# Nine of the third token block's twelve gated units computed from split operands, with the weight splits and the attention steps moved to fit

## The chip, the cores and the metric

The kernel runs on one core of a Trainium2 chip. The metric is device time in microseconds (us); lower is better. The core has a matrix engine (TensorE, PE in the profile; PEld is its weight load), a vector engine (VectorE, DVE), an activation engine (ScalarE, ACT), a general engine (GpSimd, POOL) and a queue that issues DMA transfers (SyncE, SP). Each takes its instructions in the order in which the program wrote them, and they wait for each other by semaphores.

## What is computed

The reference is an attention block with polynomial features, followed by a gated feed-forward block. The inputs are float64 in memory and arrive as pairs of 32-bit words.

```python
# attention: q, k, v are (4, 4, 1088, 32); S1, S2 are (8, 32)
phi(x) = outer(S1 @ x, S2 @ x)                 # 64 features of each token
kv = sum_s phi(k)_s v_s ;  z = sum_s phi(k)_s
attn = (phi(q) @ kv) / (phi(q) . z + 1e-6)
x = attn as (4352, 128)                        # heads side by side
# feed-forward: w_gate, w_val are (128, 1536); w_out is (1536, 128)
g = x @ w_gate
out = (g * sigmoid(g) * (x @ w_val)) @ w_out
```

## The kernel before

The 4352 tokens are cut into blocks: the first 1088 (batch 0) into three blocks, 0, 1 and 2, of 384, 320 and 384 tokens, the rest into blocks of up to 480. The 1536 hidden columns are twelve chunks of 128, so a block is twelve units (i, j): block i, chunk j. A unit multiplies the block's tokens with the gate and the value weights of its chunk, and joins the two results to a hidden tile. A down product (`down`, its matmul is L1077) multiplies a hidden tile with the chunk of `wo` and adds it to the block's sum in PSUM.

There are two forms of a unit:

- A plain unit (`unit`, L1025) is two float32 matmuls, then a Silu on ACT (L1029) and a product on DVE (L1040).
- A unit of parts (`start_unit` and `finish_unit`) splits tokens and weights into a high part, a scaled low part and their difference, and does six matmuls in the type fp32r: two of the differences (L989), a scaling of the PSUM pair on ACT (L992), four more on top (L1001, L1002), Silu (L1004) and product (L1009). The two sums of one unit lie in a pair of PSUM banks. There are three such pairs; `pair` takes the one that is longest unused and not held. A started unit holds its pair until its product.

For the second form the weights must have been split. The weights are cut for this into four groups of three chunks, called chunk 0 to 3 in the change: `cut_weights` makes g0 to g3 (gate) and v0 to v3 (value). Each is a generator of four steps: the high part on ACT (L843), the low part on DVE or POOL (L846), its scaling on ACT (L848), the difference on DVE (L851) or POOL (L855). `cut_tokens` splits the tokens of a block (ACT L865, DVE L873, DVE or POOL L868). `at` runs the next step of the ones named, and the tables `steps_at` say behind which unit or down product.

The weights themselves come as 64-bit words by DMA and are turned into float32 by `narrow` (DVE L263, L264, ACT, DVE L271, L277, POOL or DVE L286). The dictionary `parts` says behind which unit each such step is written.

The attention of batches 1 to 3 is one generator, `attentions`, and `parts_of(n)` advances it by n steps. For batch 1 the steps are: transposes of keys and queries (L327, L578, with the next batch's loads on SP), key products (L354), features on DVE (L377), their sums `zs` on POOL (L547), and in one step the key-value products (L388), the key products of batch 2 (L354), the products with `zs` (L713), a fold on DVE (L601 to L608) and the rotated copies `spread` by DMA (L729, L730). Then come the query sketches (L342), the query features and their transposes (DVE L377, L758), and last `numerators` (L776), which uses two PSUM pairs and writes the tokens of batch 1 (copies L793), the first that block 3 (`HEAD`) needs.

The order of the work around the change is written by hand, in one stream for each engine:

1. The loop over `seq` writes the plain units, index z. From z = 17 each is followed by a down product and one attention step. `lates` are hidden tiles whose product was put off; `catch_up` does it later.
2. The loop over n writes `ND` down products with attention steps, weight splits and the split of block 2's tokens ("x") between them.
3. The loop over j writes block 2's units of parts, each with a down product: start of unit j + 1, finish of unit j, down product.
4. The `while` loop writes the down products left. In it stand the numerators, the split of block 3's tokens and, with two down products left, the start of block 3's first unit.
5. Blocks 3 and on run in the loop over y, all in units of parts.

Of the kernel before, what the change touches and what calls it, by code (L numbers as in the profile page):

```python
# [19 lines left out]
def kernel(  # L20
# [28 lines left out]
    nc = tc.nc  # L49
    P = nc.NUM_PARTITIONS  # L50
# [8 lines left out]
    NCH = Dff // P  # L59
# [73 lines left out]
    def let_go(keep):  # L133
        i = kept.pop(keep)
        held.discard(i)
        touch(i, i + 1)
# [13 lines left out]
    wg = const.tile([P, NCH, P], FP32, name="wg")  # L150
    wv = const.tile([P, NCH, P], FP32, name="wv")
# [162 lines left out]
    slots = [(hbuf[:, k, :] if k < NH - NL else late[:, k - NH + NL, :]) for k in range(NH)]  # L314
# [482 lines left out]
    HEAD = len(steps)  # L797
    hidden = {}
    acc = {}
    todo = []  # L800
# [16 lines left out]
    def whole(ap):  # L817
        return ap.bitcast(FP32)
# [10 lines left out]
    def home(w, c):  # L829


        if w is wg:
            return [big("phq", k) if k < 4 else big("raw", k - 4) for k in range(3 * c, 3 * c + 3)]
        return [
            stage.tile([P, 3, P], F32R, tag=tag, name=name, bufs=6)[:]
            for tag, name in (("exp", "w1"), ("man", "wb"), (("exp", "man")[c % 2], "wd"))
        ]

    def cut_weights(w, c, low, engine):

        w1, wb, wd = w_parts[id(w), c] = home(w, c)
        src = w[:, 3 * c : 3 * c + 3, :]
        nc.scalar.activation(out=w1, in_=src, func=AF.Copy, scale=CUT)  # L843
        yield
        low = low[0]
        engine.tensor_tensor(out=low, in0=src, in1=whole(w1), op=ALU.subtract)  # L846
        yield
        nc.scalar.activation(out=wb, in_=low, func=AF.Copy, scale=BETA)  # L848
        yield
        if engine is nc.vector:  # L850
            nc.vector.scalar_tensor_tensor(  # L851
                out=wd, in0=low, scalar=-BETA, in1=whole(w1), op0=ALU.mult, op1=ALU.add
            )
        else:
            engine.tensor_tensor(out=wd, in0=whole(w1), in1=whole(wb), op=ALU.subtract)  # L855

    def cut_tokens(i, engine=nc.gpsimd, soon=False):

        t0, n = blocks[i]
        x = xT[:, t0 : t0 + n]  # L860
        x1, x0, xd = x_parts[i] = [
            apool.tile([P, WB], F32R, tag=tag, name=name, bufs=2)
            for tag, name in (("qb", "x1"), ("dT", "x0"), ("rd", "xd"))
        ]
        nc.scalar.activation(x1[:, 0:n], x, AF.Copy, scale=CUT)  # L865
# [33 lines left out]
    def now(where, y):  # L899
        for f in where.pop(y, ()):  # L900
            f()
# [81 lines left out]
    def start_unit(i, j):  # L983

        n = blocks[i][1]
        xd = x_parts[i][2][:, 0:n]
        ps = sums_of[i, j] = pair((i, j))[:, :, 0:n]
        for k, w in enumerate((wg, wv)):
            nc.tensor.matmul(  # L989
                ps[:, k], w_parts[id(w), j // 3][2][:, j % 3, :], xd, start=True, stop=True  # L990
            )
        nc.scalar.activation(ps, ps, AF.Copy, scale=-1.0 / WHOLE)  # L992

    def finish_unit(i, j, y=None):
        n = blocks[i][1]
        x1, x0, _ = (x[:, 0:n] for x in x_parts[i])
        ps = sums_of.pop((i, j))
        now(before, y)
        for k, w in enumerate((wg, wv)):
            w1, wb = (w_parts[id(w), j // 3][t][:, j % 3, :] for t in range(2))  # L1000
            nc.tensor.matmul(ps[:, k], w1, x1, start=False, stop=False, skip_group_check=True)  # L1001
            nc.tensor.matmul(ps[:, k], wb, x0, start=False, stop=True, skip_group_check=True)  # L1002
        sg = fpool.tile([P, WB], FP32, tag="sg", name="sg", bufs=5)[:, 0:n]
        nc.scalar.activation(sg, ps[:, 0], AF.Silu, scale=WHOLE)  # L1004
        slot_of[i, j] = slots.pop(0)
        hj = slot_of[i, j]
        hidden[i, j] = hj
        todo.append((i, j))
        nc.vector.scalar_tensor_tensor(  # L1009
            out=hj[:, 0:n], in0=ps[:, 1], scalar=WHOLE, in1=sg, op0=ALU.mult, op1=ALU.mult  # L1010
        )
        let_go((i, j))
        now(behind, y)
        if (i, j) in DOWN:
            cut_hidden(y, i, j)
# [135 lines left out]
    def part(name, i):  # L1151

        next(fills[name, i], None)
# [38 lines left out]
    order = [c for p in (c0, aside, c1) for c in range(*p)]  # L1192
# [8 lines left out]
    n = steps[0][1]  # L1201
# [92 lines left out]
    def free(c):  # L1294
        return [room[:, c, :].rearrange("p (c f) -> p c f", f=P)]

    w = ("wg", "wv")
    parts = {}
    for z, p in enumerate(both(3, *w) + both(4, *w) + [("wo", i) for i in range(4)]):
        z += z // 2 * 4  # L1300
        for t in (z, z + 1, z + 2 + z % 6):
            parts.setdefault(t, []).append(p)
    seq = [(0, 3), (0, 4), (0, 5), (2, 0), (2, 1), (2, 2)]
    seq += [(i, j) for i in (1, 2) for j in range(3, 6)]
    seq += [(i, j) for j0 in (6, 9) for i in (0, 1) for j in range(j0, j0 + 3)]
    order = [(0, j) for j in range(NCH)] + [(1, j) for j in range(3, NCH)] + [(1, j) for j in range(3)]

    lows = {}  # L1310
    cuts = {"x": cut_tokens(2, nc.vector, soon=True)}
    for c in (2, 3, 0, 1):
        cuts["g%d" % c] = cut_weights(wg, c, free(8 + c % 2), nc.vector if c else nc.gpsimd)
        lows["v%d" % c] = free(6 + c % 2)
        cuts["v%d" % c] = cut_weights(wv, c, lows["v%d" % c], nc.vector if c == 1 else nc.gpsimd)

    def at(*names):
        for name in names:
            next(cuts[name], None)
# [4 lines left out]
            todo.insert(0, order.pop(0))  # L1324
        down()

    steps_at = {20: ("v2",), 21: ("v3", "v2", "v3"), 22: ("g2",), 23: ("g3",)}
    for z, (i, j) in enumerate(seq):
        if z == 17:
            free_banks.pop()  # L1330
            turn[0] %= 4
        unit(i, j)
        for p in parts.get(z, ()):
            part(*p)
        if z == 6:
            load_k(1)
            load_v(1, [nc.sync] * 4)
            load_q(1)
        if z >= 17:
            next_down()  # L1340
            parts_of(1)
        if z == 19:
            catch_up(nc.vector)
            catch_up(nc.vector)
        at(*steps_at.get(z, ()))


    steps_at = {
        0: ("g2", "v2", "v3"), 1: ("g2",), 2: ("g2", "g3"), 3: ("g3", "v2"), 4: ("g3", "v3"), 5: ("g2",),
        7: ("x",), 8: ("x", "g3", "v0"), 9: ("g0",),  # L1350
    }
    ND = 13
    for n in range(ND):
        if n == ND - 2:
            start_unit(2, 6)
        next_down()
        parts_of(n in (0, 1, 7, 10, 11, 12))
        at(*steps_at.get(n, ()))
        if n == 9:
            catch_up(nc.vector)  # L1360


    steps_at = {
        7: ("v0", "g0"), 9: ("v0", "g0"), 10: ("v0", "g0"), 11: ("v1", "g1", "v1", "g1"),
    }
    todo.sort(key=lambda x: (order + [x]).index(x))
    for j in range(6, NCH):
        if j + 1 < NCH:
            start_unit(2, j + 1)
        finish_unit(2, j)  # L1370
        next_down()
        parts_of(1)
        if j == 7:


            lows["v0"][:] = [slots.pop().rearrange("p (c f) -> p c f", f=P)]
        at(*steps_at.get(j, ()))
# [89 lines left out]
```

## Time and profile before

| what | value |
|---|---|
| median of 3 runs | 277.18 us (276.96 to 277.44) |
| the profiled execution | 276.96 us |
| its span, first to last instruction | 275.2 us |
| PE busy | 269.1 us, 98% of the span |
| DVE busy | 209.7 us, 76% |
| ACT busy | 191.9 us, 70% |
| POOL busy | 101.0 us, 37% |
| mean granted TensorE clock | 0.998 |

A row of the timeline gives start, length, engine, line, operation, output and inputs, the count of instructions and, in brackets, the engine's idle time before it with what ended it. A float32 matmul of this kernel shows as two rows (x2), one of fp32r as one. A row of the chain of waits gives start, length and the piece of work. A row of the table by stretch gives the stretch, its length, the busy time of PE, PEld, DVE, ACT and POOL with the number of instructions, the granted clock, the DMA share and GB/s.

### The profile page before, as it was taken

To read this page: it belongs to the slowest core of one execution; us is meant where nothing else is said; L and a number is where in the kernel's file an instruction comes from. 1 tells how busy PE (TensorE), PEld (TensorE's weight loads), DVE (VectorE), ACT (ScalarE), POOL (GpSimd) and SP (SyncE) were. 2 spreads that over 40 slices of the span, in tenths; PEclk is the share of its full clock that TensorE was granted. 3 is DMA by queue.
4 is the path that set the end of the run, shared out by engine and by line. 5 is a ranking of instruction groups with operands and counts; after the bars stand their busy time and mean duration, and the time that the engine had idled before them with its cause. 6 is when DMAs were issued, how large, how long until landed. Compare 5 with 4: busy or idle time off the path is not lost.

```text
span 275.2 us, 5762 instructions
## 1 busy us (share of the span) xinstructions
PE 269.1 (98%) x2187; PEld 199.8 (73%) x2187; DVE 209.7 (76%) x369; ACT 191.9 (70%) x345; POOL 101.0 (37%) x113
## 2 busy tenths in 40 slices
PE   7899999999999999999999999999999999999995
PEld 7645566666785777777577777867887888788994
DVE  3997988989798773887545666967977995978771
ACT  3468566372685686677478898768879878897880
POOL 3314422159250630260043353435425553543320
PEclk9999999999999999999999999999999999999999
DMA  6673196222231043000200020000100200010021
GB/s 192 171 225 90 35 277 194 77 87 77 48 92 18 4 113 98 2 0 1 38 13 4 4 36 0 0 2 12 25 2 0 36 1 0 15 23 1 5 33 29
DMA packets 26139, 14.30 MB, mean 52 GB/s; under 512 B 19840, under 2 KB 24192, under 8 KB 26112
## 3 DMA queue, kind: packets, MB, share of 16 engines
q1 hardware_dynamic: 25456, 13.84, 19.5%
q8 instruction: 17, 0.28, 0.4%
q10 hardware_dynamic: 656, 0.10, 0.2%
q14 instruction: 10, 0.08, 0.1%
HBM read 11.41 MB, written 2.23 MB: 50 GB/s over the span
## 4 chain that ended last, share of the span: by engine, by line
PE 93%; DVE 3%; DMA 2%; ACT 1%; issue 0%; SPq 0%
PE PS L1077 21%; PE PS L1001 14%; PE PS L989 14%; PE PS L1002 14%; PE PS L1025 12%; PE PS L1072 3%; PE PS L1069 3%; PE PS L1071 3%; PE PS L354 2%; PE PS L776 2%; PE PS L342 2%; PE PS L388 2%; DMA kld<-in_k_dram 2%; PE PS L1117 1%; PE PS L497 1%; PE PS L445 1%
## 5 line engine op out<-in xcount | busy, mean ns | idle before, releaser
L992 ACT ACTIVATE PS<-PS 128x960 f32<-128x960 f32 (+1 forms) x90 | 83.3, 926 | 31.9 <-PE PS L989 31.0
L1009 DVE SCALAR_TENSOR_TENSOR hbuf<-PS,sg 128x480 f32<-128x480 f32 (+1 forms) x87 | 55.3, 636 | 41.1 <-ACT sg L1004 39.0
L1004 ACT ACTIVATE sg<-PS 128x480 f32<-128x480 f32 (+1 forms) x90 | 49.6, 551 | 1.6 <-PE PS L1002 1.2
L1077 PE MATMUL PS<-hbuf,wo 128*128 128x480 f32 (+2 forms) x94 | 39.4, 516 | 0.0
L989 PE MATMUL PS<-xd,graw 128*128 128x480 f32 (+1 forms) x69 | 37.7, 546 | 0.0
L989 PE MATMUL PS<-xd,wd 128*128 128x480 f32 (+1 forms) x90 | 33.5, 372 | 0.0
L1002 PE MATMUL PS<-x,wb 128*128 128x480 f32 (+1 forms) x90 | 33.5, 372 | 0.0
L1001 PE MATMUL PS<-x,w 128*128 128x480 f32 (+1 forms) x90 | 33.4, 371 | 0.0
L1002 PE MATMUL PS<-x,graw 128*128 128x480 f32 (+1 forms) x69 | 25.5, 370 | 0.0
L989 PEld LDWEIGHTS PS<-xd,wd 128*128 128x128 f32 x90 | 17.0, 189 | 10.3 <-issue 5.8
L1025 PE MATMUL PS<-xT,wg 128*128 128x384 f32 (+1 forms) x60 | 23.5, 474 | 0.1
L1025 PE MATMUL PS<-xT,wv 128*128 128x384 f32 (+1 forms) x60 | 23.2, 467 | 0.3 <-DVE wv L286 0.3
L1077 PEld LDWEIGHTS PS<-hbuf,wo 128*128 128x128 f32 x94 | 17.6, 189 | 5.4 <-issue 0.4
L868 POOL TENSOR_TENSOR x<-xT,x 128x480 fp32r<-128x480 f32 (+1 forms) x6 | 7.2, 1192 | 38.1 <-ACT x L865 38.1
L1077 PE MATMUL PS<-hbuf,scaled 128*128 128x480 f32 (+1 forms) x48 | 20.6, 518 | 0.0
L1029 ACT ACTIVATE sg<-PS 128x384 f32<-128x384 f32 (+1 forms) x24 | 11.2, 468 | 13.2 <-PE PS L1025 12.3
L989 PEld LDWEIGHTS PS<-xd,graw 128*128 128x128 f32 x69 | 13.0, 188 | 7.7 <-ACT PS L992 4.1
L969 POOL TENSOR_TENSOR hlate<-hbuf,hlate 128x480 fp32r<-128x480 f32 (+1 forms) x12 | 14.3, 1198 | 11.3 <-ACT hlate L968 9.2
L1001 PEld LDWEIGHTS PS<-x,w 128*128 128x128 f32 x90 | 16.9, 187 | 2.2
L1002 PEld LDWEIGHTS PS<-x,wb 128*128 128x128 f32 x90 | 16.9, 188 | 2.1
L1001 PE MATMUL PS<-x,graw 128*128 128x480 f32 (+1 forms) x48 | 18.0, 376 | 0.0
L1025 PEld LDWEIGHTS PS<-xT,wv 128*128 128x128 f32 x60 | 11.2, 190 | 7.3 <-DVE hbuf L1040 0.8
(203 smaller groups left out, 555.2 us busy)
## 6 DMA issues: line engine op xcount, KB each, us to landing
kld<-in_k_dram SPq DMA_DIRECT2D x4, 544.0 KB, 4.2
vld<-in_v_dram SPq DMA_DIRECT2D x12, 144.0 KB, 4.0
qld<-in_q_dram SPq DMA_DIRECT2D x3, 544.0 KB, 4.9
raw<-in_moe_w_out_dram SPq DMA_DIRECT2D x4, 384.0 KB, 4.3
raw<-in_moe_w_gate_dram SPq DMA_DIRECT2D x3, 384.0 KB, 3.6
raw<-in_moe_w_val_dram SPq DMA_DIRECT2D x3, 384.0 KB, 3.8
out_dram<-o SPq DMA_DIRECT2D x16, 60.0 KB, 2.0
vld<-in_v_dram SPq DMA_DIRECT2D x4, 112.0 KB, 3.9
```

Of the source, the lines that this page charges most:

```text
L969: add_to(before, y + 2, lambda: nc.gpsimd.tensor_tensor(out=h0, in0=h, in1=whole(h1), op=ALU.subtract))
L989: nc.tensor.matmul(ps[:, k], w_parts[id(w), j // 3][2][:, j % 3, :], xd, start=True, stop=True)
L992: nc.scalar.activation(ps, ps, AF.Copy, scale=-1.0 / WHOLE)
L1001: nc.tensor.matmul(ps[:, k], w1, x1, start=False, stop=False, skip_group_check=True)
L1002: nc.tensor.matmul(ps[:, k], wb, x0, start=False, stop=True, skip_group_check=True)
L1004: nc.scalar.activation(sg, ps[:, 0], AF.Silu, scale=WHOLE)
L1009: nc.vector.scalar_tensor_tensor(out=hj[:, 0:n], in0=ps[:, 1], scalar=WHOLE, in1=sg, op0=ALU.mult, op1=ALU.mult)
L1025: nc.tensor.matmul(o[:, 0:n], w[:, j, :], xT[:, t0 : t0 + n], start=True, stop=True)
L1029: nc.scalar.activation(sg[:, 0:n], g[:, 0:n], AF.Silu)
L1069: nc.tensor.matmul(acc[i][:, 0:n], wd, hd, **sides)
L1071: nc.tensor.matmul(p, w1, h1, start=(j == mine[0]), stop=False)
L1077: nc.tensor.matmul(acc[i][:, 0:n], w, hidden[i, j][:, 0:n], **sides)
```

## The change

Block 2 had six plain units (chunks j = 0 to 5) and six of parts (6 to 11). It gets three plain ones (0 to 2) and nine of parts (3 to 11).

- `seq` loses the units (2, 3), (2, 4), (2, 5): it has 21 entries, not 24. The parts of `wo` that were to be converted behind z = 21 and 22 now stand behind the first down products.
- Ahead of the first finish of a unit of parts stand 23 down products (four in the loop over `seq` and 19 in the loop over n), not 20 (seven and 13). Their order interleaves blocks 0 and 1.
- The weight groups are split in the order 1, 2, 3, 0, not 2, 3, 0, 1. All gate groups use DVE; the value groups 1, 2, 3 use POOL, group 0 uses DVE. Before, g0, v0, v2 and v3 used POOL and the others DVE.
- The attention steps are spread anew. The step that reads `zs` stands behind the twelfth down product of the loop over n (before: behind the eighth), the query sketches behind the fourteenth.
- The numerators and the split of block 3's tokens stand in front of the finish of unit (2, 11), not behind it among the last down products. Four down products are left behind that unit, of which the first belongs to its own iteration; the start of block 3's first unit still stands two down products before the end.

```diff
-    seq = [(0, 3), (0, 4), (0, 5), (2, 0), (2, 1), (2, 2)]
-    seq += [(i, j) for i in (1, 2) for j in range(3, 6)]
+    seq = [(i, j) for i in (0, 2, 1) for j in ((3, 4, 5), (0, 1, 2))[i == 2]]
     seq += [(i, j) for j0 in (6, 9) for i in (0, 1) for j in range(j0, j0 + 3)]
-    order = [(0, j) for j in range(NCH)] + [(1, j) for j in range(3, NCH)] + [(1, j) for j in range(3)]
+    order = [(i, j) for i in (0, 1) for j in range(3 * i, 6)]
+    order += [(i, j) for j0 in (6, 9) for i in (0, 1) for j in range(j0, j0 + 3)] + [(1, j) for j in range(3)]
...
-    for c in (2, 3, 0, 1):
-        cuts["g%d" % c] = cut_weights(wg, c, free(8 + c % 2), nc.vector if c else nc.gpsimd)
+    for c in (1, 2, 3, 0):
         lows["v%d" % c] = free(6 + c % 2)
-        cuts["v%d" % c] = cut_weights(wv, c, lows["v%d" % c], nc.vector if c == 1 else nc.gpsimd)
+        cuts["g%d" % c] = cut_weights(wg, c, free(8 + c % 2), nc.vector)
+        cuts["v%d" % c] = cut_weights(wv, c, lows["v%d" % c], nc.gpsimd if c else nc.vector)
...
-    steps_at = {20: ("v2",), 21: ("v3", "v2", "v3"), 22: ("g2",), 23: ("g3",)}
...
-        for p in parts.get(z, ()):
+        for p in parts.pop(z, ()):
             part(*p)
...
         if z == 19:
-            catch_up(nc.vector)
-            catch_up(nc.vector)
-        at(*steps_at.get(z, ()))
+            for _ in range(3):
+                catch_up(nc.vector)
+        if z == 20:
+            at("v1", "v2")
...
     steps_at = {
-        0: ("g2", "v2", "v3"), 1: ("g2",), 2: ("g2", "g3"), 3: ("g3", "v2"), 4: ("g3", "v3"), 5: ("g2",),
-        7: ("x",), 8: ("x", "g3", "v0"), 9: ("g0",),
+        0: ("v1", "v2"), 1: ("g1",), 2: ("g2",), 3: ("g1", "v1", "v2"), 4: ("g1",), 5: ("g1", "g2"), 6: ("g2", "v1"),
+        7: ("g2", "v2"), 8: ("v3",), 9: ("g3",), 10: ("v0",), 11: ("g0",), 12: ("x",), 13: ("x",), 14: ("g3",),
+        15: ("g3",), 18: ("g3",),
     }
-    ND = 13
+    ND = 19
     for n in range(ND):
         if n == ND - 2:
-            start_unit(2, 6)
+            start_unit(2, 3)
         next_down()
-        parts_of(n in (0, 1, 7, 10, 11, 12))
+        for p in parts.pop(len(seq) + n, ()):
+            part(*p)
+        parts_of(n in (0, 1, 2, 3, 4, 11, 13, 15, 16, 17))
         at(*steps_at.get(n, ()))
-        if n == 9:
-            catch_up(nc.vector)
...
+    steps_at = {4: ("v3",), 6: ("v3",), 7: ("v3",), 8: ("v0", "g0"), 9: ("v0", "g0"), 10: ("v0", "g0")}
-    for j in range(6, NCH):
+    for j in range(3, NCH):
         if j + 1 < NCH:
             start_unit(2, j + 1)
+        else:
+            parts_of(1)
+            x_steps = cut_tokens(HEAD, nc.vector, soon=True)
+            next(x_steps)
         finish_unit(2, j)
         next_down()
-        parts_of(1)
-        if j == 7:
-            lows["v0"][:] = [slots.pop().rearrange("p (c f) -> p c f", f=P)]
+        parts_of(j < 8)
+        if j == 4:
+            lows["v3"][:] = [slots.pop().rearrange("p (c f) -> p c f", f=P)]
         at(*steps_at.get(j, ()))
-    x_steps = iter(())
-    steps_at = {9: ("v1", "g1"), 8: ("v1", "g1")}
     while todo:
         if len(todo) == 2:
             start_unit(HEAD, 0)
         next_down()
-        at(*steps_at.get(len(todo), ()))
         next(x_steps, None)
-        if len(todo) == 7:
-            parts_of(1)
-            x_steps = cut_tokens(HEAD, nc.vector, soon=True)
-            next(x_steps)
-        if len(todo) in (2, 3, 4):
-            parts_of(1)
+        parts_of(len(todo) > 0)
```

More of the change, by code (lines that the diff above doesn't have):

```diff
@@ L1342 @@
         if z == 19:
-            catch_up(nc.vector)
-            catch_up(nc.vector)
-        at(*steps_at.get(z, ()))
+            for _ in range(3):
+                catch_up(nc.vector)
+        if z == 20:
+            at("v1", "v2")
     steps_at = {
-        0: ("g2", "v2", "v3"), 1: ("g2",), 2: ("g2", "g3"), 3: ("g3", "v2"), 4: ("g3", "v3"), 5: ("g2",),
-        7: ("x",), 8: ("x", "g3", "v0"), 9: ("g0",),
+        0: ("v1", "v2"), 1: ("g1",), 2: ("g2",), 3: ("g1", "v1", "v2"), 4: ("g1",), 5: ("g1", "g2"), 6: ("g2", "v1"),
+        7: ("g2", "v2"), 8: ("v3",), 9: ("g3",), 10: ("v0",), 11: ("g0",), 12: ("x",), 13: ("x",), 14: ("g3",),
+        15: ("g3",), 18: ("g3",),
     }
-    ND = 13
+    ND = 19
     for n in range(ND):
         if n == ND - 2:
-            start_unit(2, 6)
+            start_unit(2, 3)
         next_down()
-        parts_of(n in (0, 1, 7, 10, 11, 12))
+        for p in parts.pop(len(seq) + n, ()):
+            part(*p)
+        parts_of(n in (0, 1, 2, 3, 4, 11, 13, 15, 16, 17))
         at(*steps_at.get(n, ()))
-        if n == 9:
-            catch_up(nc.vector)
-    steps_at = {
-        7: ("v0", "g0"), 9: ("v0", "g0"), 10: ("v0", "g0"), 11: ("v1", "g1", "v1", "g1"),
-    }
+    steps_at = {4: ("v3",), 6: ("v3",), 7: ("v3",), 8: ("v0", "g0"), 9: ("v0", "g0"), 10: ("v0", "g0")}
     todo.sort(key=lambda x: (order + [x]).index(x))
-    for j in range(6, NCH):
+    for j in range(3, NCH):
         if j + 1 < NCH:
             start_unit(2, j + 1)
+        else:
+            parts_of(1)
+            x_steps = cut_tokens(HEAD, nc.vector, soon=True)
+            next(x_steps)
         finish_unit(2, j)
         next_down()
-        parts_of(1)
-        if j == 7:
-            lows["v0"][:] = [slots.pop().rearrange("p (c f) -> p c f", f=P)]
+        parts_of(j < 8)
+        if j == 4:
+            lows["v3"][:] = [slots.pop().rearrange("p (c f) -> p c f", f=P)]
         at(*steps_at.get(j, ()))
-    x_steps = iter(())
-    steps_at = {9: ("v1", "g1"), 8: ("v1", "g1")}
     while todo:
```

## The prediction

> **What bounds the kernel now.** I read the page's first parts, then the chain of waits, then the timeline of all engines from 46 to 92 us (the stretch the change rewrites), and tables of that stretch cut into pieces.
>
> ```profile
> PE 269.1 (98%) x2187; PEld 199.8 (73%) x2187; DVE 209.7 (76%) x369; ACT 191.9 (70%) x345; POOL 101.0 (37%) x113
> PE 93%; DVE 3%; DMA 2%; ACT 1%; issue 0%; SPq 0%
> ```
>
> TensorE (PE) sets the end; a microsecond less on PE is a microsecond gained only while nothing makes PE wait. From the chain of waits (start, length, piece):
>
> ```profile
> 49.12 1.29 PE PS L1025 x4
> 50.41 0.65 PE PS L1077 x2
> ...
> 66.33 1.14 PE PS L388 x72
> 67.47 1.20 PE PS L354 x36
> ...
> 75.02 0.54 PE PS L1077 x2
> 76.60 0.54 PE PS L1077 x2
> 78.18 0.54 PE PS L1077 x2
> ```
>
> A plain unit of 384 tokens (L1025) is 1.29 us. A down product (L1077) is 0.65 for 384 tokens, 0.54 for 320. A unit of parts (six matmuls, L989, L1001, L1002) is the period less the down: 1.58 - 0.54 = 1.04 us. The pieces are contiguous: PE hardly waits. But beside it, by stretch (PE, PEld, DVE, ACT, POOL busy):
>
> ```profile
> 58.00:64.00 6.00, 6.00 (x22) 3.78 (x21) 5.91 (x10) 2.52 (x6) 4.96 (x6) 1.00 0.29 93
> 64.00:70.00 6.00, 6.00 (x129) 4.44 (x128) 5.74 (x12) 2.67 (x7) 5.76 (x6) 1.00 0.37 109
> ```
>
> VectorE (DVE) and GpSimd (POOL) are full there. They make block 1's key sums `zs`, which PE reads at L713, and the timeline shows the hand-over:
>
> ```profile
> 60.61 0.55 DVE L277 SCALAR_TENSOR_TENSOR man<-raw,man 128x384 f32<-128x384 uint32 x1
> 61.23 1.01 POOL L286 TENSOR_TENSOR wo<-man,exp 128x384 f32<-128x384 f32 x1 [0.96 <-DVE man L277]
> 62.19 1.28 POOL L547 TENSOR_TENSOR zs<-phk 128x512 f32<-128x512 f32 x1
> 63.55 2.81 POOL L547 TENSOR_TENSOR zs<-zs,phk 128x512 f32<-128x512 f32 x2
> 66.44 0.93 POOL L547 TENSOR_TENSOR zs<-zs 128x256 f32<-128x256 f32 x1
> 67.45 0.93 POOL L547 TENSOR_TENSOR zs<-zs,phk 128x256 f32<-128x256 f32 x1
> 68.60 0.32 PE L713 MATMUL PS<-zs,ones 128*32 128x64 f32 x8
> ```
>
> `zs` is ready at 67.45 + 0.93 = 68.38; PE gets there at 68.60. The cover is 0.22 us. Last, the end of unit (2,10), from the same timeline:
>
> ```profile
> 81.01 0.81 ACT L992 ACTIVATE PS<-PS 128x768 f32<-128x768 f32 x1
> 81.18 0.81 PE L1077 MATMUL PS<-hbuf,wo 128*128 128x384 f32 x2
> 81.74 0.49 ACT L1004 ACTIVATE sg<-PS 128x384 f32<-128x384 f32 x1
> 82.26 0.56 DVE L1009 SCALAR_TENSOR_TENSOR late<-PS,sg 128x384 f32<-128x384 f32 x1
> ```
>
> PE ends the down behind (2,10) at 81.99; the unit's PSUM pair is free only at 82.82, because ScalarE (ACT) came late.
>
> **What the Trainium skill says.** "FP8 and Floating Point Precision", TensorE Precision Notes: true fp32 takes four passes. Agrees: 0.645 us for 384 columns at L1077 against 1.04 / 6 = 0.173 at the fp32r parts. "TensorE: Matmul & The Clock Gate", Architectural detail: ScalarE and VectorE are strict FIFOs, GpSimd too. Agrees: each engine's starts follow the program's order, and the POOL sums stood behind wo's L286. "GPSIMD Engine Reference", Specifications: GpSimd shares SBUF interfaces with VectorE, and VectorE instructions with two SBUF inputs contend. Agrees: the DVE subtraction L846 took 1.20 and 1.08 us beside POOL's sums, 0.52 alone.
>
> **The change, part by part.**
>
> *Units.* Three units (2,3) to (2,5) turn from plain into parts: 3 x (1.29 - 1.04) = -0.75 us on PE (-0.77 unrounded). ACT gains three scalings L992 of 0.80 = 2.4 us; in 70 to 82 us it had 3.4 us free, and they spread over nine periods of 1.68 us with 1.28 of ACT work each: no cost unless something else stands in ACT's queue (below). DVE's product only moves from L1040 (0.55) to L1009 (0.56).
>
> *Front of the stage.* Up to the unit with z = 17 both kernels run twelve 384 and six 320 units: same 48.48 us. The later weights (wg, wv of piece 3 ready at 35.7, used from 37; piece 4 at 42.8, used from 44.6) are still in time. Before, PE then did six units and 15 downs ahead of L713; now three (1,9..11) and 16. So PE's arrival moves by -3 x 1.29 = -3.87, and downs from 12 x 0.645 + 3 x 0.54 = 9.36 to 10 x 0.645 + 6 x 0.54 = 9.69, +0.33: 68.60 - 3.54 = 65.06.
>
> *The sums.* They do not move up as much. The last wo piece's L277 stands ahead of them on DVE, its L286 and the two v subtractions L846 (1.96 together) on POOL. DVE from the product of z = 17 (48.85) to that L277's end (61.16) had 1.37 us idle (0.44, 0.22, 0.71), which goes, since PE feeds it earlier. Its work loses two 320 products (0.40 each in succession) and 3 x 0.07 for the smaller sizes, gains 0.07 and one catch-up (0.42): -0.52. It starts 0.45 later, as z = 17 is now a 384 unit behind the wo conversions. Together 1.44 earlier: L277 ends at 59.7, `zs` at 66.95. POOL is free for it: wo's third L286 at 56.5, the v subtractions until 59.5. **PE waits at L713 for 66.95 - 65.06 = 1.85, say 1.8 us.** Bounds: 1.0 if POOL's sums lose their contention (0.75 instead of 0.93 for the small ones, 1.33 for 1.40) and DVE has a lucky order; 2.6 if DVE gains nothing but its idle time. No gain is possible. The key transposes L327 (DVE 63.9) and key product L354 need no wait. Behind L713 on PE stand everything else and, on DVE, fold L601, which the sketches L342 need: fold's chain takes 0.9 us, two downs (1.29) cover it.
>
> *Weight splits.* g1, v1, g2, v2 now precede the first parts unit where g2, v2, g3, v3 did: same counts, on the same engines. ACT's w1 steps for v3, g3, v0, g0 come earlier, where ACT is free. v3's low part (POOL, at j = 4) to wd (POOL, at j = 7) ends about 81.2 for a use at 81.4: 0.2 of cover, taken as nothing, up to 0.4 if POOL runs at 1.2 instead of 1.0. v0 and g0 go from POOL to DVE: 4 x 0.55 = 2.2 us, at j = 8 and 10, where DVE has no more attention steps: hidden; else 0.5.
>
> *SP and DMA.* Block 1's six spread copies and four v loads now go ahead of block 0's four stores, not behind. Spread's six issues took 71.12 to 75.4 and land within 3 us; read at 86: hidden. The key, query loads stay behind the same transposes, used 10 us later.
>
> *Numerators.* They (L776, 1.48 us, 64 matmuls) stood four downs behind the last unit. Now they stand right behind (2,10)'s down, with (2,11)'s pair held; of three pairs they need the other two, one of which is (2,10)'s. Before's row gives the price: free at 82.82, PE there at 81.99: 0.83 and a semaphore. ACT's backlog is the same (two wb steps of 0.53 in front of L992), with 0.1 more period to drain. **0.85 us**; bounds 0.4 and 1.3. Behind it: token split for the next block (ACT copy, x1, DVE xd) took 2.2 us from numerators' end; PE has the rest of (2,11), 0.69, and three downs, 1.94: 2.63 of cover. Nothing.
>
> Sum: -0.77 + 1.80 + 0.85 = **+1.9 us**. The profiled execution took 276.96 (span 275.2 and 1.76 around it), so 278.85; the median is 0.22 above that: **279.0**. From the next block on both run the same rows, PE-bound, so the shift stays.
>
> **Rivals.**
> *A third wait, 280.3.* ACT's wb of g3 stands ahead of the scaling of (2,3), and waits for a DVE subtraction behind xd, a store's transpose and x0. I find it ready at 71.9, PE wanting the scaling from 72.2. For: DVE ops beside POOL took 1.19 (xd) instead of 0.55; two such are 1.3 us late. Against: POOL's wd steps should be over by 69.2. Decides if that subtraction ends after 72.2.
> *Only the numerators wait, 277.3.* If `zs` is early (65.1), -0.77 + 0.85. For: DVE loses the three products near the sums. Against: 1.85 us to make up with both engines full.
> *Faster, 276.4.* The sums decide it alone: with `zs` done by 65.1 all that DVE and ACT do behind L713 also starts 1.8 us earlier against PE, and this lead drains ACT's backlog by (2,10). Then only -0.77 stays. Against: ACT's backlog at (2,10) arises on the spot, from wb steps bound to j = 9. It needs L713's wait under about 0.2.
> That the change fails to do what it says I can rule out: the order of instructions has nine units and the downs as told.
>
> **How the numbers follow.** Both waits (277.9 to 280.1): 0.58. Third wait (up to 281): 0.16. Numerators only: 0.13, within 0.2%. Faster: 0.13. A measurement of this kernel can tell about 0.2%, 0.55 us, from no change. Chances: faster 0.13, same 0.13, slower 0.74. The range, 276.6 to 280.6, leaves out half of the faster case and the worst third waits; the likeliest case alone is 277.9 to 280.1.
>
> **What would show it.** POOL's last L547 ending near 67 and L713 starting just behind it, with PE idle over 1 us; L776's third or fourth matmul waiting for L1009 of (2,10); unit periods of 1.68 without gaps; the first L989 with 480 columns 1.5 to 2 us later than 90.34. Wrong if L713 starts at 65 without a wait, if PE waits at the first parts unit, or if PE's arrival at L713 is not 3.5 us earlier.

## The result and the profile after

| what | before | after |
|---|---|---|
| median of 4 runs | 277.19 us (276.96 to 277.44) | 281.36 us (279.75 to 281.51) |
| the profiled execution | 276.96 us, span 275.2 | 279.75 us, span 278.0 |

The ratio is 1.0137, 95% interval 1.0099 to 1.0175. The forecast was 279.0 (276.6 to 280.6): slower, as said, but the time lies above the range. The profiled execution is the fastest of the four. In it the granted TensorE clock is 1.0; in the other three it is 0.994 on average and the span is 1.6 to 1.8 us longer. So there are two questions: 2.8 us in the profiled execution where 1.9 were forecast, and 1.6 more in most others.

First the page of after, its busy times and the shares of the chain that ended last:

```profile
PE 269.6 (97%) x2193; PEld 201.4 (72%) x2193; DVE 213.7 (77%) x371; ACT 193.9 (70%) x348; POOL 99.2 (36%) x111
PE 86%; DVE 7%; POOL 2%; DMA 2%; issue 1%; ACT 1%; SPq 0%; DVEq 0%; ACTq 0%; POOLq 0%
```

PE is busy for as long as before (269.1 us), though it has 0.77 us less to do: a wait that falls between the matmuls of the numerators counts as busy here. Its share of the chain falls from 93% to 86%: DVE and POOL have got in. The view of waits of PE's weight loads, from 40 to 104 us (us in total, times, longest), names three places:

```profile
PEld PS L713 <- POOL zs L547: 2.0, 1, 2.0
PEld PS L354 <- DVE kT L327: 1.1, 2, 0.5
...
PEld PS L989 <- DVE hbuf L1009: 0.6, 1, 0.6
```

These are waits of the weight load, which runs ahead of PE; what PE lost is the idle time in the timeline. This is the timeline of after around the sums:

```profile
57.70 2.26 POOL L846 TENSOR_TENSOR room<-wv,w 128x384 f32<-128x384 f32 x2
58.04 1.07 DVE L271 SCALAR_TENSOR_TENSOR exp<-raw,exp 128x384 int32<-128x384 int32 x1
59.03 1.36 DVE L277 SCALAR_TENSOR_TENSOR man<-raw,man 128x384 f32<-128x384 uint32 x1
...
64.40 0.70 DVE L327 STREAM_TRANSPOSE kT<-kld 128x512 f32<-128x512 f32 x1
...
65.15 0.69 PE L354 MATMUL PS<-s,kT 128*64 128x64 f32 x16 [0.41 <-DVE kT L327]
...
66.69 0.92 POOL L547 TENSOR_TENSOR zs<-zs,phk 128x256 f32<-128x256 f32 x1
...
67.66 0.32 PE L713 MATMUL PS<-zs,ones 128*32 128x64 f32 x8 [1.82 <-POOL zs L547]
```

PE stands still twice in front of the fold: 0.41 us for the second half of the key transposes, which DVE does late, and 1.82 us for `zs`. Where the last `wo` conversion (L271, L277) runs beside POOL's two subtractions L846, it takes 1.07 and 1.36 us; beside an idle POOL, two conversions earlier in the same kernel, it took 0.55 each. In the trace of before only its first half stood beside these subtractions (58.31 to 60.27). Its L277 there is shown in the prediction, with 0.55 us; its L271 is this one:

```profile
59.63 1.05 DVE L271 SCALAR_TENSOR_TENSOR exp<-raw,exp 128x384 int32<-128x384 int32 x1
```

The end of the stage is in the chain of waits of after:

```profile
87.72 2.36 PE PS L776 x41
...
92.10 0.55 DVE hbuf L1009
...
93.21 2.69 DVE phk L377 x4
...
96.91 0.66 DVE hbuf L1009
...
97.61 0.48 PE PS L989
...
100.28 0.73 PE PS L388 x41
```

The numerators L776 take 2.36 us where they took 1.48, and the four features L377 3.86 where they took 2.76. The line of the numerators in the chain of before, then the features and what follows them in its timeline, then the features of after:

```profile
85.42 1.48 PE PS L776 x38
```

```profile
89.58 2.76 DVE L377 TENSOR_TENSOR phk<-kab 128x768 f32<-128x768 f32 x4
...
94.07 0.66 DVE L1009 SCALAR_TENSOR_TENSOR hbuf<-PS,sg 128x480 f32<-128x480 f32 x1 [1.73 <-ACT sg L1004]
```

```profile
93.13 3.86 DVE L377 TENSOR_TENSOR phk<-kab 128x768 f32<-128x768 f32 x4
```

Behind the numerators the chain leaves PE: the token copy, the token split, the product of unit (2,11), the four key features L377 and block 3's first product stand in one queue on DVE, and the L989 at 97.61 needs the last of them. PE works on other things meanwhile, and waits 0.23 us.

The sum, on PE. The program's early units start 0.09 us later in this trace; that is taken off, except in the last row.

| step | forecast | measured |
|---|---|---|
| three units become units of parts | -0.77 | -0.77 (periods 1.69, less 0.65 for the down: 1.04) |
| wait for the second key transposes (L354) | 0 | +0.41 |
| wait for `zs` (L713) | +1.80 | +1.82 |
| wait of the numerators (L776) | +0.85 | +0.88 |
| start of block 3, first 480-column L989 (89.88 before, 92.38 after, both in the timeline) | +1.9 | +2.41 |
| from there to the key-value products L388 (97.48 before, 100.28 after) | 0 | +0.30 |
| from L388 to the end of the span (177.7 in both) | 0 | 0 |
| span | +1.9 | +2.8 |

### The profile page after: what moved, and what is told of

It reads as the page before. It is cut to its first block, busy times and chain, and to the rows that moved or that the text cites. A ratio compares the mean times of both kernels' runs of the same rounds, so it can differ in the third digit from the quotient of the medians.

```text
span 278.0 us, 5775 instructions
## 1 busy us (share of the span) xinstructions
PE 269.6 (97%) x2193; PEld 201.4 (72%) x2193; DVE 213.7 (77%) x371; ACT 193.9 (70%) x348; POOL 99.2 (36%) x111
## 3 DMA queue, kind: packets, MB, share of 16 engines
HBM read 11.41 MB, written 2.23 MB: 49 GB/s over the span
## 4 chain that ended last, share of the span: by engine, by line
PE 86%; DVE 7%; POOL 2%; DMA 2%; issue 1%; ACT 1%; SPq 0%; DVEq 0%; ACTq 0%; POOLq 0%
PE PS L1077 17%; PE PS L1001 14%; PE PS L989 14%; PE PS L1002 13%; PE PS L1025 10%; PE PS L1069 3%; PE PS L1072 3%; PE PS L1071 3%; PE PS L776 2%; PE PS L342 2%; POOL zs L547 2%; DMA kld<-in_k_dram 2%; PE PS L354 1%; DVE phk L377 1%; PE PS L388 1%
## 5 line engine op out<-in xcount | busy, mean ns | idle before, releaser
L992 ACT ACTIVATE PS<-PS 128x960 f32<-128x960 f32 (+1 forms) x93 | 85.7, 922 | 33.0 <-PE PS L989 32.0
L1009 DVE SCALAR_TENSOR_TENSOR hbuf<-PS,sg 128x480 f32<-128x480 f32 (+1 forms) x93 | 58.5, 629 | 40.5 <-ACT sg L1004 38.3
L1004 ACT ACTIVATE sg<-PS 128x480 f32<-128x480 f32 (+1 forms) x93 | 51.1, 549 | 1.3 <-PE PS L1002 1.2
L1077 PE MATMUL PS<-hbuf,wo 128*128 128x480 f32 (+2 forms) x100 | 41.6, 518 | 0.0
L989 PE MATMUL PS<-xd,graw 128*128 128x480 f32 (+1 forms) x72 | 39.9, 554 | 0.0
L989 PE MATMUL PS<-xd,wd 128*128 128x480 f32 (+1 forms) x93 | 34.5, 371 | 0.2 <-DVE hbuf L1009 0.2
L1001 PE MATMUL PS<-x,w 128*128 128x480 f32 (+1 forms) x93 | 34.4, 370 | 0.0
L1002 PE MATMUL PS<-x,graw 128*128 128x480 f32 (+1 forms) x72 | 26.6, 369 | 0.0
L989 PEld LDWEIGHTS PS<-xd,wd 128*128 128x128 f32 x93 | 17.6, 189 | 11.3 <-issue 5.9
L1025 PE MATMUL PS<-xT,wg 128*128 128x384 f32 (+1 forms) x54 | 21.1, 472 | 0.1
L1025 PE MATMUL PS<-xT,wv 128*128 128x384 f32 (+1 forms) x54 | 20.7, 466 | 0.3 <-DVE wv L286 0.3
L989 PEld LDWEIGHTS PS<-xd,graw 128*128 128x128 f32 x72 | 13.6, 189 | 8.1 <-ACT PS L992 4.1
L1001 PEld LDWEIGHTS PS<-x,w 128*128 128x128 f32 x93 | 17.5, 188 | 2.2
L1001 PE MATMUL PS<-x,graw 128*128 128x480 f32 (+1 forms) x48 | 18.1, 376 | 0.0
L1029 ACT ACTIVATE sg<-PS 128x384 f32<-128x384 f32 (+1 forms) x21 | 9.6, 462 | 11.1 <-PE PS L1025 11.1
L1001 PE MATMUL PS<-x,gphq 128*128 128x480 f32 (+1 forms) x45 | 17.0, 377 | 0.0
```

Source lines behind the costliest of these rows:

```text
L989: nc.tensor.matmul(ps[:, k], w_parts[id(w), j // 3][2][:, j % 3, :], xd, start=True, stop=True)
L1009: nc.vector.scalar_tensor_tensor(out=hj[:, 0:n], in0=ps[:, 1], scalar=WHOLE, in1=sg, op0=ALU.mult, op1=ALU.mult)
L1025: nc.tensor.matmul(o[:, 0:n], w[:, j, :], xT[:, t0 : t0 + n], start=True, stop=True)
L1029: nc.scalar.activation(sg[:, 0:n], g[:, 0:n], AF.Silu)
L1077: nc.tensor.matmul(acc[i][:, 0:n], w, hidden[i, j][:, 0:n], **sides)
```

## The experiments

All are edits of the changed kernel. "Before" ran beside each; its medians were 277.31 (11 runs), 277.33 (23), 277.10 (11) and 277.17 (19).

The theory ahead of the experiments: the time is PE waiting at three places (the sums, the numerators, the DVE queue behind them), and the slower executions are a fall of the clock caused by the first of them. The rivals: the clock falls for a reason outside these waits; the waits are of one chain, so that taking one away lengthens the next.

**The changed kernel again** (no edit).

> The changed kernel once more, to see its spread and where the clock goes. Theory (idle PE): the 1.8 us of idle PE ahead of the key sums' products L713, after 2.4 us of small matmuls, lets the clock gate drop for a stretch in some executions; so times lie in two groups, about 279.7 (clock 1.0) and 281.4 (clock 0.994), and a trace of the slower group shows the granted clock under 1 only between 66 and 74 us. Rival (elsewhere): the clock falls at the start of the kernel or around the numerators near 88 us. Rival (chance): the clock has nothing to do with the change, and this run is at 279.7 throughout.

280.77 us (279.88 to 281.82, 4 runs), ratio 1.0103 (1.0057 to 1.0148). With the first four there are eight executions: three at clock 0.999 to 1.0 with 279.75 to 280.15 us, five at 0.993 or 0.994 with 281.29 to 281.82. The means are 1.56 us apart.

**Matmuls in the wait for the sums.** The eight added matmuls write to an unused part of PSUM and feed no output.

```diff
         run_copies(copies, 2)
+        keep_warm(8, ps=kvz[:, 1, :])
         value_sums(kvz[:, 0, :], zs)
```

> Eight matmuls of 512 columns without use, 1.7 us, stand ahead of L713 and fill the wait for the key sums; nothing else changes, and they feed no output. Theory (idle PE): the wait itself stays, the clock does not fall any more, every execution at about 279.8 and clock 1.0. Rival (elsewhere or chance): still two groups, most at 281.4 with clock 0.994. If the fill takes longer than the wait, up to 0.3 us more.

280.04 us (279.76 to 280.29, 5 runs), ratio 1.0069 (1.0039 to 1.0099); the clock was 0.998 or more in all five. Two lines of its timeline (a line number is one higher behind the edit, so L714 is L713):

```profile
66.07 1.91 PE L241 MATMUL PS<-const-bfloat16-1.0 128*32 128x512 bf16 x8
67.96 0.32 PE L714 MATMUL PS<-zs,ones 128*32 128x64 f32 x8
```

PE is busy until `zs` is there, no sooner than in the changed kernel. The slower executions are gone, the wait's own time is not. So what was lost beyond the profiled execution comes from PE standing still in front of L713. By counts alone this is not strong: if the matmuls changed nothing, five executions in a row without a fall would come up about once in 23, worked out from the five of eight. The traces that follow say the same.

**One feature step of batch 2 moved out of the queue** behind the numerators, into block 3's loop.

```diff
-        parts_of(len(todo) > 0)
+        parts_of(len(todo) > 1)
```

> One of the three feature steps of batch 2 behind the numerators (512 elements on DVE) goes from the last down products to block 3's loop; nothing else. Theory (DVE chain behind the late numerators): the product of block 3's first unit comes 0.6 to 1.0 us earlier, at about 96, start of its fourth unit waits 0.2 instead of 0.6, span 277.4 to 277.7 at clock 1.0. Rival (PE bound there): no change, 278.0. Rival (moved): key sums of batch 2 come later, and L713 near 102 waits.

281.49 us (279.85 to 281.59, 4 runs), ratio 1.0124 (1.0093 to 1.0155). No gain: PE's wait for L1009 moves one unit on. But this profile is of an execution at 0.994, and shows where the clock falls. One line of its table by stretch (stretch, length; PE, PEld, DVE, ACT, POOL busy; granted clock, DMA share, GB/s), and then its chain of waits:

```profile
68.00:72.00 4.00, 4.00 (x52) 2.32 (x56) 2.77 (x9) 2.24 (x6) 1.84 (x2) 0.57 0.08 21
```

```profile
67.98 2.76 PE PS L1077 x4
70.75 1.97 PE PS L342 x72
...
74.53 0.35 PE PS L989 x2
```

The same piece of the chain of the changed kernel, at clock 1.0:

```profile
67.98 1.49 PE PS L1077 x4
69.47 1.62 PE PS L342 x72
...
72.90 0.35 PE PS L989 x2
```

The stretch has a mean clock of 0.57; the four us before and behind it have 1.00. In finer steps the clock is half from 68.0 to 71.5. In both traces L713 starts at 67.66. Right behind it two down products take 2.76 us in place of 1.49, and the sketches 1.97 in place of 1.62; then all is as it was. The first unit of parts starts 1.63 us later, about the distance between the two groups of executions, and about half of the 3.4 us. This fits the Trainium skill, "TensorE: Matmul & The Clock Gate", Part 1, What's actually happening: a gate passes half of the clock's pulses after an idle window of about 3.4 us, and its window runs freely, so where it falls differs from run to run. The length agrees: 3.4 us here. The page asks for an idle window, though; here PE was idle for 2.2 us of the 3.4 before, and five of eight executions fell.

Three more of the profiled executions below have such a stretch: numerators, step two (half clock from 68.7 to 72.1 us), later products, less far (71.5 to 74.9), and products three downs later (70.7 to 77.5, twice the length). It begins in a gap of PE or within 0.8 us of its end, also where the gap has moved. In the 3.4 us ahead of the four falls PE was idle for 2.2, 1.9, 1.7 and 1.8 us. So about half of such a stretch was enough here; one gap of 1.1 us is not half. This is read from four traces, and no run was made to test it.

**The products with `zs` three downs later**, and all attention steps behind them with them.

```diff
-        parts_of(n in (0, 1, 2, 3, 4, 11, 13, 15, 16, 17))
+        parts_of(n in (0, 1, 2, 3, 4, 14, 16, 17, 18))
...
-        parts_of(j < 8)
+        parts_of(j < 9)
```

> The attention step with L713 stands three down products later (n = 14 instead of 11), the sketches two (n = 16), the query steps after them likewise, and end at j = 8 instead of 7. Theory (sums late): PE arrives 1.83 us later at L713, the 1.8 us wait and the 0.4 us at the key transposes go, with them the fall of the clock: 277.4 to 278.0, clock 1.0, L713 waits under 0.3 us. Rival (the loss lies at numerators and behind): under 0.7 us gained on 279.75. Rival (moved, not removed): L342 or the first units of parts take the wait, 279 or more.

282.85 us (282.30 to 283.90, 4 runs), ratio 1.017 (1.0126 to 1.0213): slower still. Its view of waits, first line:

```profile
PEld PS L342 <- DVE s L608: 3.2, 1, 3.2
```

The wait for `zs` fell from 2.0 to 0.7 in this view of weight loads, but the fold, which begins with L713 on PE, now stands on DVE behind the token split of block 2 and a store's transpose, which wait for others. The sketches L342 wait 3.2 us for it. The clock fell in all four executions (0.988 to 0.994).

**Later products, less far** (two downs), with the token split kept behind the fold.

```diff
-        7: ("g2", "v2"), 8: ("v3",), 9: ("g3",), 10: ("v0",), 11: ("g0",), 12: ("x",), 13: ("x",), 14: ("g3",),
-        15: ("g3",), 18: ("g3",),
+        7: ("g2", "v2"), 8: ("v3",), 9: ("g3",), 10: ("v0",), 11: ("g0",), 13: ("x",), 14: ("x",), 15: ("g3",),
+        16: ("g3",), 18: ("g3",),
...
-        parts_of(n in (0, 1, 2, 3, 4, 11, 13, 15, 16, 17))
+        parts_of(n in (0, 1, 2, 3, 4, 13, 15, 16, 17, 18))
```

> The earlier try at a later L713, mended: only the places of the attention steps change, L713 behind down product n = 13 (not 11), the sketches n = 15, the query steps 16 to 18, and the token split x, which had stood ahead of the fold on DVE in that try, goes to n = 13 and 14. Theory (PE is early, the sums late): PE arrives 1.29 us later, L713 waits 0.5 instead of 1.8, L354 for the key transposes not at all, L342 not over 0.5: 1.3 to 1.7 us gained, 278.1 to 278.5, nearly all executions at clock 0.998 or more. Rival (moved): the wait turns up at L342 or at the first units of parts, 279.3 or more.

279.7 us (279.44 to 282.31, 4 runs), ratio 1.0109 (1.0072 to 1.0146): a miss. PE's idle times in its trace are 1.15 us at L713 and 0.72 at L342, 1.87 together for the 2.23 of the changed kernel. Two downs more ahead of L713 (1.08 us) filled part of its wait, but the store's transpose (0.57 us) got ahead of the fold on DVE, and the fold's last step L608 took 0.96 us instead of 0.35, beside POOL's L855 in both traces: the sketches were late. The three executions at 0.998 or more (279.44 to 279.75) are some 0.3 better than the changed kernel's three, as these idle times are. The profiled execution, 282.31, has the half clock behind L342, and was late for a further reason: its first key products L354 took 2.19 us instead of 1.49, long before the place of the change.

**POOL's subtractions out of the last `wo` conversion's way**: the low parts of v1 and v2 behind the sums, that of g1 behind the second key transpose.

```diff
-        0: ("v1", "v2"), 1: ("g1",), 2: ("g2",), 3: ("g1", "v1", "v2"), 4: ("g1",), 5: ("g1", "g2"), 6: ("g2", "v1"),
-        7: ("g2", "v2"), 8: ("v3",), 9: ("g3",), 10: ("v0",), 11: ("g0",), 12: ("x",), 13: ("x",), 14: ("g3",),
+        1: ("g1",), 2: ("g2",), 3: ("v1", "v2"), 4: ("g1",), 5: ("g1",), 6: ("g1", "g2"), 7: ("g2",), 8: ("g2", "v3"),
+        9: ("g3",), 10: ("v0",), 11: ("g0",), 12: ("x", "v1", "v2"), 13: ("x",), 14: ("g3", "v1", "v2"),
```

> The two subtractions of v1 and v2 on POOL (2.26 us together) go behind the key sums instead of ahead of them, their later steps to n = 12 and 14; the low part of g1 on DVE goes behind the second key transpose instead of between the two. Theory (POOL and DVE queues make the sums late): the last wo conversion loses its contention (L271 1.07 and L277 1.36 fall to 0.55 each), the sums end about 1.3 us earlier, near 66.2; L354 waits no more, L713 waits 0.5 to 1.0 instead of 1.8; 278.2 to 278.8 at clock 1.0, and most executions at clock 1.0. Rival (DVE features bound the sums): they end less than 0.4 us earlier. Rival (moved): the first unit of parts waits for v1's difference, no gain.

279.15 us (278.65 to 280.16, 4 runs), ratio 1.0064 (1.0040 to 1.0089); clock 0.998 or more in all four. Its timeline:

```profile
58.74 0.55 DVE L277 SCALAR_TENSOR_TENSOR man<-raw,man 128x384 f32<-128x384 uint32 x1
...
66.56 0.32 PE L713 MATMUL PS<-zs,ones 128*32 128x64 f32 x8 [1.11 <-POOL zs L547]
```

L271 and L277 take 0.54 and 0.55 us again, the sums start and end 1.1 us earlier (1.35 if this execution's later start is taken off, which is what the two instructions gained, 1.34), the gap at L354 is gone and that at L713 is 1.11. So the two moves together, POOL's and that of g1, were worth 1.1 us of the 2.23 of idle time. With half of it gone, no execution of the four lost its clock; four are few.

**The numerators, step one**: ACT's scalings of v0 and g0 one unit later, behind the numerators.

```diff
-    steps_at = {4: ("v3",), 6: ("v3",), 7: ("v3",), 8: ("v0", "g0"), 9: ("v0", "g0"), 10: ("v0", "g0")}
+    steps_at = {4: ("v3",), 6: ("v3",), 7: ("v3",), 8: ("v0", "g0"), 10: ("v0", "g0")}
...
         else:
+            at("v0", "g0")
             parts_of(1)
```

> The scaling step of v0 and g0 (two ACT steps of 0.53) moves from j = 9 to j = 10, behind the Silu of unit (2,10), and their last step on DVE ahead of the numerators' copies. Theory (ACT backlog): Silu and product of (2,10) come 0.9 us earlier, the wait inside L776 falls from 0.88 to under 0.2, and the time by about 0.8: 279.0 at clock 1.0, 280.6 at 0.994. Rival (pair not the cause): L776 still takes 2.3 us. Rival (shifted): start of block 3 waits for the wd steps instead, no gain.

280.98 us (279.54 to 281.53, 7 runs), ratio 1.0105 (1.0073 to 1.0138). L776 takes 2.11 us in place of 2.36: ACT's backlog was 0.25 of the 0.88. The rest is unit (2,10) itself, whose Silu and product follow its last matmul.

**Step two**: a down product between unit (2,10)'s and the numerators, and block 3 started one down later. The last loop has one turn less for it, so one feature step also goes to block 3's loop; alone, above, that gained nothing.

```diff
         else:
+            next_down()
+            at("v0", "g0")
             parts_of(1)
...
-        if len(todo) == 2:
+        if len(todo) == 1:
             start_unit(HEAD, 0)
```

The scalings stay as in step one.

> One more down product stands ahead of the numerators, the scaling of v0 and g0 moves to j = 10, block 3 starts with one down product left instead of two, and with one turn of the last loop gone one feature step of batch 2 goes to block 3's loop. Theory (the pair of (2,10)): L776 takes 1.5 instead of 2.36, and with the shifted feature step the span falls by 1.2 to 1.6, to 276.5 to 276.8 at clock 1.0. Rival (token split not covered): block 3's first start waits 0.3 or more, gain under 0.6. Rival (only the feature step counts): same as the run with that step alone.

280.1 us (278.77 to 281.08, 4 runs), ratio 1.0091 (1.0059 to 1.0123). The two executions at clock 1.0 took 278.77 and 279.46, the two at 0.994 took 280.75 and 281.08. L776 is at 1.48 us again and no PE gap is left behind it. Against the changed kernel's executions of like clock that is 0.4 to 1.2 us.

**Both repairs** (POOL's and the numerators').

> Both changes together: sums first on POOL, numerators one down product later, one feature step later. Theory (waits add): 278.0 less 1.2 to 1.5 less 1.2 to 1.6, a span of 275.0 to 275.6, times of 276.7 to 277.4: level with the kernel before or up to 0.2% under it, of whose 0.77 us saved 0.5 to 1.0 stays lost at L713. Rival (waits do not add): over 277.6.

278.1 us (277.88 to 279.81, 18 runs), ratio 1.0038 (1.0022 to 1.0053). Of PE's gaps only 1.10 us at L713 are left. The time is over the 277.6 that was to speak for waits that don't add, but that mark rested on larger single gains than were measured. The traces decide it. The second key-value products L388 (100.28 in the changed kernel), with each execution's later start and in step two the 1.62 us of half clock taken off, come 1.02 us earlier with POOL's repair, 0.91 with the numerators', and 1.93 with both. The gains add: the waits are separate, not one chain.

**Both repairs and the products with `zs` two downs later**, and with them the token split and what is left of the splits of v1, v2 and g3. The diff is against the kernel with both repairs, and each of the two that follow is against this one.

```diff
-        9: ("g3",), 10: ("v0",), 11: ("g0",), 12: ("x", "v1", "v2"), 13: ("x",), 14: ("g3", "v1", "v2"),
-        15: ("g3",), 18: ("g3",),
+        9: ("g3",), 10: ("v0",), 11: ("g0",), 13: ("x", "v1", "v2"), 14: ("x",), 15: ("g3", "v1", "v2"),
+        16: ("g3",), 18: ("g3",),
...
-        parts_of(n in (0, 1, 2, 3, 4, 11, 13, 15, 16, 17))
+        parts_of(n in (0, 1, 2, 3, 4, 13, 15, 16, 17, 18))
```

> The best kernel so far with L713 and the sketches two down products later. Theory (waits add): its 1.2 us wait at L713 goes, 276.8 to 277.1, 0.1 to 0.2% under the kernel before; of the 0.77 us saved some 0.4 is left. Rival (moved): L342 waits for the fold or unit (2,3) for its tokens, 277.6 or more.

277.69 us (277.51 to 278.08, 5 runs), ratio 1.0016 (0.9996 to 1.0036). The wait at L713 is gone, 0.61 us at L342 has come (for `s`, as in the run two downs later without repairs; L608 takes 0.96 us again), and one first part waits for an L1009 that stands behind a query feature on DVE.

**With block 3 started at two downs left**, as in the changed kernel.

```diff
-        if len(todo) == 1:
+        if len(todo) == 2:
             start_unit(HEAD, 0)
```

> The same, with block 3's first unit started with two down products left, not one. Theory A (ACT's scaling late with one left, 0.4 us): 0.1 to 0.3 faster than the version with one. Theory B (token split not ready): start waits 0.2 to 0.4 for xd, level or slower.

278.35 us (278.21 to 279.76, 6 runs), ratio 1.0048 (1.0026 to 1.0071). The weight load of L989 now waits 0.7 us for the token split's `xd`, of which PE loses some 0.3, and PE stands still for 0.53 us for an L1009 behind a feature. The down product taken from behind the numerators is cover that the token split needs.

**The sketches and all query steps one place later.**

```diff
-        16: ("g3",), 18: ("g3",),
+        18: ("g3",),
...
-        parts_of(n in (0, 1, 2, 3, 4, 13, 15, 16, 17, 18))
+        parts_of(n in (0, 1, 2, 3, 4, 13, 16, 17, 18))
...
-    steps_at = {4: ("v3",),
+    steps_at = {3: ("g3",), 4: ("v3",),
...
-        parts_of(j < 8)
+        parts_of(j < 9)
```

> The kernel with both repairs and the sums' products at down 13 (g_late) still loses 0.61 us at L342 (waits for s) and 0.4 us at a first part of a unit (L989 waits for L1009 of (2,3), behind a query feature L377 on DVE). Here the query sketches and all query steps behind them come one down or unit later, and g3's last two steps stand behind the scaling of (2,3). Theory (those two waits are all that eats the units' 0.77 us): both gone, key-value products of batch 2 at 97.1 to 97.4 against 97.48 before, measured from the same start; 276.6 to 277.0. Rival (the work in front of L342's results is in order on ACT and DVE, so the wait goes to the scaling L992 of (2,3) or to the first unit's parts): 277.5 to 277.9, level with g_late.

277.07 us (276.81 to 278.70, 14 runs) beside 277.17 for the kernel before; ratio 1.0008 (0.9994 to 1.0021). Its timeline between 30 and 104 us shows one gap of PE, and its chain of waits the small ones left:

```profile
70.81 0.44 PE L989 MATMUL PS<-xd,wd 128*128 128x384 f32 x1 [0.17 <-POOL wd L855]
```

```profile
87.85 0.39 PE PS L1001
...
92.24 0.48 PE PS L1001
...
97.39 1.14 PE PS L388 x72
```

The theory expected L388 at 97.1 to 97.4 and found 97.37 from the same start, 0.11 us ahead of the kernel before. This fits the 0.77 us of the units: 0.17 at `wd`, 0.22 where the first L1001 behind the numerators takes 0.39 instead of 0.17, and 0.26 where block 3's first takes 0.48 instead of 0.22 stand against it, and -0.77 + 0.65 is -0.12. The trace of before has small losses of this kind too (an L1001 of 0.33 at 81.99), so the account closes to about 0.1 only. So nine units of parts can be had at no loss, but what they save goes to waits of about 0.2 us each. No version here beats the kernel before.

Two of the fourteen executions, 278.64 and 278.70, have a clock of 0.994, though this kernel's trace has no PE gap over 0.17 us after 30 us. So have three of the 68 of the kernel before (278.92 to 278.94). A fall of the clock therefore also comes without the waits, only seldom; the waits made it 13 of 23 in the four kernels that keep them both (changed, feature step, numerators one and two).

## Why the prediction was right in direction and wrong in size

**Units, right.** -0.77 us, by the periods of 1.69; the sum of the last experiment fits it.

**The front of the stage, right to 0.3.** Without its two gaps PE would have come to L713 at 65.3; the forecast said 65.06.

**The sums, right in kind, 0.4 too small.** Two statements failed. "Key transposes L327 ... and key product L354 need no wait": they cost 0.41. "L277 ends at 59.7, `zs` at 66.95": L277 ended at 60.3 and `zs` at 67.5, taken from the same start. The forecast gave DVE's work at this place its old durations. Before, L271 ran beside POOL's subtractions and L277 behind them, 1.60 us together; now both run beside them and take 2.43, 0.83 more. That is enough for the 0.6 by which L277 was late. It had named the contention (the Trainium skill, "GPSIMD Engine Reference", Specifications: shared SBUF interfaces) for the subtractions beside the sums, and did not ask what else the moved POOL work would run beside. The run with POOL's work moved away shows it: 0.55 each, and 1.1 us of PE's idle time gone. That the wait at L713 came out at 1.82 for 1.80 is partly luck: PE and `zs` were each some 0.6 later than forecast.

**The numerators, right.** 0.88 for 0.85, by the product L1009 of unit (2,10), whose Silu comes behind the scaling L992 on ACT, as named. That ACT's backlog is what makes them wait was too much said: moving the backlog away gave 0.25 back.

**"Behind it ... Nothing", wrong by 0.3.** The forecast compared PE's cover of 2.63 us with the token split's 2.2, and this was right: the first start of block 3 didn't wait. (Five down products stand behind unit (2,11), not four as the description of the change has it; three of them are this cover.) It stopped there. On DVE the product of (2,11), the low part of the tokens and the four key features L377 stand next, then block 3's first product. The features took 3.86 us, where before they took 2.76: the last of them took 1.79 beside POOL's first sum. Before, it ran beside that sum too and took 0.68, and the sum took 1.88 instead of 1.61; why DVE lost this time is not shown. Before the change the features ended 1.7 us ahead of that product; now they end with it. The statement that the shift stays from the next block on is right from L388 on.

**The clock, no term at all.** "The median is 0.22 above that" took from the kernel before that its executions are alike. The wait makes them differ: 1.6 us more in five of eight. With the matmuls in the wait five executions had no such difference, and the traces show the half speed behind the waits. This is the larger part of the error in the median; the range would have held the profiled execution's 279.75.

**The rivals.** No third wait came: the first units of parts run without a gap, so the rival that ended at 280.3 isn't what made the time. "Numerators only" and "faster" needed `zs` by 65.1.

The step that failed first is therefore the price of the wait at L713: right as an idle time, and too cheap by what idle time does to the clock, a term put at nothing that measured 1.6 us. The second is the 0.9 us in the profiled execution: 0.41 at L354 and 0.3 behind the numerators, both put at nothing, and the rest in terms under 0.1.

## What to carry to other kernels

Where work moves on POOL, look up every DVE instruction that it will now run beside, and allow for a longer duration than the one it has alone. Where a step is set closer to its neighbours, follow the whole queue of each engine behind it up to the next thing that PE needs, not only the first. A new idle time of TensorE of about 2 us cost this kernel its length, and 1.6 us more in 13 of 23 executions; count both, and fill such a gap with other matmuls or shorten it.

## What the runs showed of the hardware

- TensorE fell to half speed after idle times of 0.41 and 1.82 us within 2.9 us, in 13 of 23 executions, for 3.4 us. With one gap of 1.11 us it did so in none of four executions (POOL's repair) and with one of 1.10 in two of eighteen (both repairs, clock 0.992). The last kernel, with no gap over 0.17, fell in two of fourteen and the kernel before in three of 68, so a gap of 1.1 us is not shown to matter. No trace shows where the clock fell in these.
- The four stretches of half clock that were traced are 3.4 us long, or twice that, and PE had been idle for 1.7 to 2.2 of the 3.4 us ahead of each.
- DVE instructions with two inputs from SBUF slowed by more than I had seen in the trace of before: L277 took 1.36 us beside POOL's subtraction and 0.55 alone, L846 1.62 beside POOL's sums and 0.55 alone. POOL's two subtractions took 2.26 there and 1.96 before.
- Some executions of several kernels, five of 68 of the one before too (278.5 to 278.8), are about 1.4 us longer at an unchanged mean clock. One profile, that of the later products, less far, had such a start: the first key products and query products took 2.19 and 1.61 us instead of 1.49 and 0.94 at a granted clock of 1.00, and everything behind them was 1.4 us late. It is the start of the program, which the change doesn't touch. That the others are late at the same place is not shown.
